# Attention and feed-forward on one core: the second batch's heads scored with queries on the partitions, one step per tile of the first feed-forward

## The chip, the cores and the metric

One of the NeuronCores of a Trainium2 chip runs the kernel. The metric is the device time of one execution in microseconds. The kernel before took 1074.35 us, the median of three runs (1073.28 to 1077.59).

## The reference

Eight batches of eight heads: 512 local queries attend to a window of 32 positions on either side and to 32 global keys, 32 global queries attend to everything. The heads of a batch laid side by side (512 columns) are the input of a feed-forward layer with a softplus.

```python
s_g = scale * np.matmul(q_g, k_all.transpose(0, 1, 3, 2))
out_g = np.matmul(sm(s_g), v_all)
...
mask = np.abs(pos[:, None] - pos[None, :]) <= window
s_ll = np.where(mask, s_ll, -1000000000.0)
s_lg = scale * np.matmul(q_l, k_g.transpose(0, 1, 3, 2))
a_l = sm(np.concatenate([s_lg, s_ll], axis=-1))
out_l = np.matmul(a_l, np.concatenate([v_g, v_l], axis=2))
...
h = x @ w_in                                    # 4352 x 512 by 512 x 2048
g = np.maximum(h, 0.0) + np.log1p(np.exp(-np.abs(h)))
out = g @ w_out                                 # 2048 x 512
```

The weights arrive as 64-bit floats and are split on the chip.

## The kernel before

**Feed-forward.** A batch's 512 local tokens go through 16 tiles of 128 columns of d_ff. Tile f of batch b is `h{b}_{f}`: four groups of three matmuls (high and low half of x, `xh` and `xl`, against the weights `wi`), then `act` (ScalarE takes the absolute value, the exponential and the logarithm; VectorE puts the softplus together in `e`; ScalarE casts its high half `gh`; GpSimd subtracts the low half `gl`). The second product adds tile f into four banks `o{b}_{t}` (three matmuls each, against `wo`), and it stands one or two tiles behind. The first product has a pool of two banks (`ps_h`), so that tile f + 2 waits until VectorE has read tile f.

**Weights.** The 32 weight tiles (`wi0` to `wi15`, `wo0` to `wo15`) come as raw 512 KB blocks and are split by `split_w`: ScalarE takes an absolute value (`wbits`), VectorE does four integer steps (L486, L488, L489, L492), ScalarE casts the high half, GpSimd subtracts the low half. Twelve are put out with the first batch's attention, the other twenty during the first feed-forward. A raw block lies in the SBUF tile of the next weight.

**Attention of the first batch** (pairs of heads m = 0 to 3) has the queries on the partitions. A step is half a pair, (m, a): `scores0` (mask and scores into two banks, `s0`), `soft0` (VectorE takes the maximum along the row and scales it, ScalarE does four exponentials with their sums), `invert0` and `diag0` (the reciprocals, put on a diagonal by ScalarE), `turn0` (eight matmuls that transpose and normalise at once, `t0`), `evict0` (ScalarE copies one half of `t0`, and then VectorE the other), `values0` (`o0_{m}_{a}`) and `split0`. After each two pairs comes a step for the global queries (`s0g`, `t0g`, `o0g`).

**Attention of all other batches** (m = 4 to 31) has the keys on the partitions: `scores` in three pieces (`s_ps`), a maximum by 32 x 32 transposes on VectorE (`mt`), `maxima` across partitions, a subtraction on GpSimd, an exponential, `values` (`v_ps`), and the sums' reciprocals by way of DRAM (`combine`, `invert`, `normalise`). For m below `MPE` the mask is added on TensorE and the scores are copied by ScalarE; from there on VectorE adds it while it copies.

**Order.** The pieces of m = 4 to 31 carry due times (12 per pair), and the feed-forward's items have due times of their own; pieces are put out between items. Pieces due before `START` come ahead of the first feed-forward. The scheduler then sets each engine's order. PSUM beside `ps_h`: a pool `ps_a` with one buffer of two banks (tag `a`), for `t0`, `v_ps` and later `s_ps`; and four banks `oA`, `oB` for the first scores, which become the four banks of the second product when that begins. Loads are issued in order by SyncE; the inputs of m = 4 among them ahead of the first feed-forward.

Of the kernel before, what the change touches and what calls it, by code (L numbers as in the profile page):

```python
# [31 lines left out]
MPE = 8  # L32
# [5 lines left out]
START = 69  # L38
# [15 lines left out]
def moe_over_global_local_attention(  # L54
# [28 lines left out]
    identf = pl.tile([P, P], F32, tag="e", name="identf", bufs=2)  # L83
# [4 lines left out]
    mask0 = pl.tile([P, 2, 2, 224], BF16, tag="rb", name="mask0", bufs=1)  # L88
# [47 lines left out]
    spare = [(kind, k) for k in range(NF - 1, 9, -1) for kind in ("wo", "wi")]  # L136

    def load0(m):
        for a, w in ((0, 704), (1, 832)):
            kind, k = spare.pop()  # L140
            t = pl.tile([P, w], F32, tag=f"{kind}{k}", name=f"raw0_{m}_{a}", bufs=1)
            order["load"] = nc.sync.dma_start(out=t, in_=qk0[m, :, 704 * a:704 * a + w]).ins
            st["raw0", m, a] = t
        kind, k = spare.pop()
        t = pl.tile([P, 4, 2, P], F32, tag=f"{kind}{k}", name=f"v0_{m}", bufs=1)
        order["load"] = nc.sync.dma_start(out=t, in_=v0[m].rearrange("p (c a d) -> p c a d", c=4, a=2)).ins
        st["v0", m] = t
# [7 lines left out]
    def exps0(shape, name):  # L155
        count0.append(name)
        tag = ("x", "wi9", "x", "wo9")[len(count0) % 4]
        return pl.tile(shape, F32, tag=tag, name=f"e0_{name}", bufs=2 if tag == "x" else 1)
# [45 lines left out]

    def evict0(m, a):
        v4 = st.pop(("t0", m, a)).rearrange("p h (c k q) -> p h c k q", c=2, k=2)
        t = st["p0", m, a] = [pl.tile([P, 2, 2, P], F32, tag=g, name=f"p0_{m}_{a}{g}", bufs=3) for g in ("gh", "gl")]
        keep("act", nc.scalar.copy(t[0], v4[:, :, :, 0]))
        keep("dve", nc.vector.tensor_copy(t[1][0:96], v4[0:96, :, :, 1]))

    def values0(m, a):
        t, vt = st.pop(("p0", m, a)), st["v0", m]
        ps = st["o0", m, a] = ps_h.tile([P, 512], F32, tag="h", name=f"o0_{m}_{a}").rearrange("p (c h q) -> p c h q", c=2, h=2)
        for c in range(2):
            for k, n in enumerate((P, 96)):
                mm(ps[:, c], lhsT=vt[:n, 2 * a + c, k], rhs=t[k][:n, :, c], start=k == 0, stop=k == 1, skip_group_check=True)

    def split0(m, a):
        ps = st.pop(("o0", m, a))
        if a == 0:  # L220
            xh[m] = pl.tile([P, 512], F32R, tag=f"xh{m}", name=f"xh0_{m}", bufs=1)
            xl[m] = pl.tile([P, 512], F32R, tag=f"xl{m}", name=f"xl0_{m}", bufs=1)
        hi, lo = ([x[m][r, 256 * a:256 * a + 256].rearrange("p (c q) -> p c q", c=2) for r in (slice(0, 64), slice(64, P))] for x in (xh, xl))
        part = [ps[64 * h:64 * h + 64, :, h] for h in range(2)]
        for h in range(2):
            keep("act", nc.scalar.copy(hi[h], part[h]))
        for h in range(2):
            keep("dve", nc.vector.tensor_tensor(lo[h], part[h], hi[h].bitcast(F32), op=ALU.subtract))  # L228


    def scores0g(n):
        ps = ps_s.tile([P, 2, 512], F32, tag=("oA", "oB")[n], name=f"s0g{n}")
# [16 lines left out]
    def evict0g(n):  # L249
        ps = st.pop(("t0g", n))  # L250
        t = st["p0g", n] = [pl.tile([P, 4, P], F32, tag=g, name=f"p0g{n}{g}", bufs=3) for g in ("gh", "gl")]
# [3 lines left out]
    def values0g(n):  # L255
        t = st.pop(("p0g", n))
        ps = st["o0g", n] = ps_h.tile([P, 512], F32, tag="h", name=f"o0g{n}")
# [6 lines left out]
    def split0g(n):  # L264
# [5 lines left out]
        nc.scalar.dma_start(out=xg_dram[2 * n:2 * n + 2, :, 0:SG].rearrange("j p q -> p j q"), in_=y)  # L270
# [3 lines left out]
    def load(m, p):  # L274
        w = QW[p] + KWID[p]
        raw = pl.tile([P, 544], F32, tag="raw", name=f"raw{m}_{p}", bufs=3)
        order["load"] = nc.sync.dma_start(out=raw[:, :w], in_=qk[m - M0, :, EW[p]:EW[p] + w]).ins
        st["raw", m, p] = raw

    def load_v(m):  # L280
        t = pl.tile([P, 2, 6, 66], F32, tag="v", name=f"v{m}", bufs=2)
        nc.gpsimd.memset(t[:, :, :, D:D + 1], 1.0)
        nc.sync.dma_start(out=t[:, :, :, 0:D], in_=v[m - M0].rearrange("p (h c d) -> p h c d", h=2, d=D))
        st["v", m] = t

    def scores(m, p):
        raw = st.pop(("raw", m, p))
        q = QW[p]
        if m < M0 + 2:
            ps = ps_s.tile([P, 2, 512], F32, tag=("oA", "oB")[(3 * m + p) % 2], name=f"s_ps{m}_{p}")  # L290
        else:
            ps = ps_a.tile([P, 2, 512], F32, tag="a", name=f"s_ps{m}_{p}")
        parts = ((0, 0, 192), (192, 96, 192 if p < 2 else 96))
        pe_mask = m < MPE
        masks = (mask[:, 0:192], mask[:, 192:384] if p < 2 else mask5)
        for i, (o, qs, w) in enumerate(parts):
            ks = q + 128 * i
            for h in range(2):
                r = slice(64 * h, 64 * h + 64)
                mm(ps[:, h, o:o + w], lhsT=raw[r, ks:ks + P], rhs=raw[r, qs:qs + w],  # L300
                   start=True, stop=not pe_mask, skip_group_check=True)
            for h in range(2 if pe_mask else 0):
                mm(ps[:, h, o:o + w], lhsT=ident, rhs=masks[i], start=False, stop=True, skip_group_check=True)
# [6 lines left out]
        if pe_mask:  # L310
            nc.scalar.copy(s, ps[:, :, 0:32 * nb])
        else:
            for o, mk in ((0, mask[:, 0:384]),) if p < 2 else ((0, mask[:, 0:192]), (192, mask5)):
                w = mk.shape[1]
                nc.vector.tensor_tensor(s[:, :, o:o + w], ps[:, :, o:o + w], mk.unsqueeze(1).to_broadcast([P, 2, w]), op=ALU.add)  # L315
# [95 lines left out]
    def pieces():  # L411
# [6 lines left out]
        for m in range(M0, M):  # L418
# [20 lines left out]
    def split_x(b, j):  # L439
        xh[j] = pl.tile([P, 512], F32R, tag=f"xh{j}", name=f"xh{b}_{j}", bufs=1)  # L440
        xl[j] = pl.tile([P, 512], F32R, tag=f"xl{j}", name=f"xl{b}_{j}", bufs=1)
        if b < B:
            assert (b, j) in ready
            t, seg = xa[b, j], SEG
# [67 lines left out]
    def moe_items():  # L512
# [70 lines left out]
        for i, (b, f) in enumerate(tiles):  # L583
            if f == 0 and b > 0:
                items.append((b, 0, 0, lambda b=b: [split_x(b, j) for j in range(4)]))
            w = 0 if b else 4 * f
# [20 lines left out]
    wk = [0, 0]  # L607

    def loads(upto):
        while wk[0] < min(upto, len(order_w)):  # L610
# [4 lines left out]
    def weights(upto):  # L615
        loads(upto + AHEAD)
        while wk[1] < min(upto, len(order_w)):
# [13 lines left out]
    pcs = pieces()  # L631
    local = (scores0, lambda m, a: invert0((m, a), 4), lambda m, a: diag0((m, a), 4), turn0, evict0, values0, split0)
    glob = (scores0g, lambda n: invert0(n, 1), lambda n: diag0(n, 1), turn0g, evict0g, values0g, split0g)
    steps = [(local, (m, a)) for m in range(M0) for a in range(2)]
    for at, n in ((6, 0), (9, 1)):
        steps.insert(at, (glob, (n,)))
    n = len(steps)
# [6 lines left out]
    for k in range(-2, n + 2):  # L644
        stage(k + 2, 0)

        while k >= n - 2 and pcs[0][0] < min(12 * M0 + 8 * (k - n + 3), START):
            pcs.pop(0)[1]()
# [13 lines left out]
        if -1 <= k and wk[1] < W_PRE:  # L662
            held = order_w[wk[1]]
            held += (abs_w(*held),)
            wk[1] += 1
    tight = False
# [18 lines left out]
def _layout(q_l, k_l, v_l, q_g, k_g, v_g):  # L685
# [21 lines left out]
    cols, va, vb = [], vl[:H].reshape(H, 4, P, D), np.zeros((H, 4, P, D), v_l.dtype)  # L707
    for c in range(4):
        x0 = P * c
        before = kl[:H, :, x0 - 32:x0] if c else pad[:H]  # L710
        behind = kl[:H, :, x0 + P:x0 + P + 32] if c < 3 else pad[:H]
        cols += [ql[:H, :, x0:x0 + P], kg[:H], before, behind, kl[:H, :, x0:x0 + P]]
        vb[:, c, 0:32] = vg[:H]
        if c:
            vb[:, c, 32:64] = vl[:H, x0 - 32:x0]
        if c < 3:
            vb[:, c, 64:96] = vl[:H, x0 + P:x0 + P + 32]
    g = np.zeros((H, D, 4, 32), q_l.dtype)
    for h in range(H):
        g[h, :, h % 4] = qg[h]  # L720
    qk0 = np.concatenate(cols + [g.reshape(H, D, P)], axis=2).reshape(M0, P, 1536)
    v0 = np.stack([va, vb], axis=2).reshape(M0, 2, 4, 2, P, D).transpose(0, 4, 2, 3, 1, 5).reshape(M0, P, 1024)
    return [np.ascontiguousarray(a) for a in (qk0, v0, qk[M0:], v[M0:])]
# [20 lines left out]
```

## Time and profile before

| | |
|---|---|
| median of 3 runs | 1074.35 us (1073.28 to 1077.59) |
| the profiled execution | 1076.06 us, span 1074.0 us |
| first matmul of the first feed-forward | 89.74 us |
| first matmul of the second feed-forward | 239.41 us |
| steady length of a batch (waits for `rb` of successive batches at 470.04 and 585.94 us) | 115.90 us |

An engine's line in the profile names the source line, the engine, the operation and the tiles (written from read). In a timeline the first number is the start in us from the span's start, the second the length; `x4` says that four equal instructions are merged, and the square bracket is the idle time ahead of it with what ended it. Matmuls are pipelined, so the distance from one start to the next tells what a group costs TensorE, and not its length. A matmul of 32-bit floats counts as two instructions.

### The profile page before, as it was taken

To read this page: it belongs to the slowest core of one execution; us is meant where nothing else is said; L and a number is where in the kernel's file an instruction comes from. 1 tells how busy PE (TensorE), PEld (TensorE's weight loads), DVE (VectorE), ACT (ScalarE), POOL (GpSimd) and SP (SyncE) were. 2 spreads that over 40 slices of the span, in tenths; PEclk is the share of its full clock that TensorE was granted. 3 is DMA by queue.
4 is the path that set the end of the run, shared out by engine and by line. 5 is a ranking of instruction groups with operands and counts; after the bars stand their busy time and mean duration, and the time that the engine had idled before them with its cause. 6 is when DMAs were issued, how large, how long until landed. Compare 5 with 4: busy or idle time off the path is not lost.

```text
span 1074.0 us, 14186 instructions
## 1 busy us (share of the span) xinstructions
PE 1016.3 (95%) x5108; PEld 803.7 (75%) x5108; DVE 593.4 (55%) x1138; ACT 556.2 (52%) x998; POOL 437.2 (41%) x496
## 2 busy tenths in 40 slices
PE   6895788898999999999999999999999999999996
PEld 4674566676777777777777777777777778888895
DVE  6988697965455655565545645565556542311111
ACT  6855555454445545455445544554455554554452
POOL 2236475642444444444434344444444441122221
PEclk8998889999999999999999999999999999999999
DMA  9532332312222221223212312131212210200010
GB/s 363 166 91 99 102 133 76 97 47 85 57 49 57 82 57 48 57 58 97 57 47 58 96 46 57 49 93 45 58 48 64 79 28 13 72 1 1 1 41 20
DMA packets 78566, 75.05 MB, mean 70 GB/s; under 512 B 53380, under 2 KB 57476, under 8 KB 78496
## 3 DMA queue, kind: packets, MB, share of 16 engines
q1 hardware_dynamic: 77952, 74.09, 23.3%
q8 instruction: 40, 0.66, 0.3%
q14 instruction: 30, 0.25, 0.1%
q10 hardware_dynamic: 544, 0.07, 0.0%
HBM read 64.43 MB, written 9.71 MB: 69 GB/s over the span
## 4 chain that ended last, share of the span: by engine, by line
PE 74%; DVE 7%; DMA 4%; issue 3%; POOL 2%; ACT 1%; POOLq 0%; ACTq 0%
PE h L126 31%; PE o L126 30%; PE v_ps L126 8%; PE s_ps L126 5%; DMA rb<-rec_scratch 2%; DVE xl L452 2%; DVE xa L404 1%; DMA rec_scratch<-sc 1%; POOL s L352 1%; DVE mt L316 1%; DVE s L315 1%; POOL wo L498 0%; DVE mb L347 0%; DVE wbitswo L489 0%; DVE wbitswo L486 0%
## 5 line engine op out<-in xcount | busy, mean ns | idle before, releaser
L126 PE MATMUL h<-xh,wi 128*128 128x512 f32 (+1 forms) x1152 | 357.4, 394 | 17.0 <-DVE xl L228 9.3
L126 PE MATMUL o<-wo,gh 128*128 128x512 f32 x1088 | 346.3, 400 | 0.0
L547 POOL TENSOR_TENSOR gl<-e,gh 128x512 fp32r<-128x512 f32 x136 | 177.2, 1303 | 397.2 <-ACT gh L546 340.4
L126 PEld LDWEIGHTS h<-xh,wi 128*128 128x128 f32 x1152 | 208.7, 190 | 65.3 <-issue 16.1
L126 PEld LDWEIGHTS o<-wo,gh 128*128 128x128 f32 x1088 | 201.6, 190 | 44.3 <-issue 4.0
L126 PE MATMUL h<-xl,wi 128*128 128x512 f32 (+1 forms) x576 | 220.9, 384 | 3.6 <-DVE xl L452 3.6
L126 PE MATMUL o<-wo,gl 128*128 128x512 f32 x544 | 214.2, 394 | 0.0
L540 ACT ACTIVATE e<-h 128x512 f32<-128x512 f32 x136 | 81.3, 598 | 254.9 <-PE h L126 252.6
L543 DVE SCALAR_TENSOR_TENSOR e<-h,e 128x512 f32<-128x512 f32 x136 | 93.2, 685 | 185.5 <-ACT e L542 185.5
L352 POOL TENSOR_TENSOR s<-s,mb 128x384 f32<-128x384 f32 x112 | 137.9, 1262 | 14.0 <-DVE mb L347 14.0
L126 PEld LDWEIGHTS h<-xl,wi 128*128 128x128 f32 x576 | 109.4, 190 | 28.4 <-DVE xl L452 6.4
L546 ACT CAST gh<-e 128x512 fp32r<-128x512 f32 x136 | 83.9, 617 | 89.7 <-DVE e L543 89.6
L126 PEld LDWEIGHTS o<-wo,gl 128*128 128x128 f32 x544 | 102.8, 189 | 22.9
L126 PE MATMUL v_ps<-s,v 128*65 128x192 f32 (+1 forms) x672 | 115.4, 315 | 3.0 <-DVE s L315 2.7
L315 DVE TENSOR_TENSOR s<-s_ps,mask 128x768 f32<-128x768 f32 (+1 forms) x96 | 64.9, 696 | 82.3 <-PE s_ps L126 82.3
L126 PEld LDWEIGHTS v_ps<-s,v 128*65 128x65 f32 x672 | 89.7, 138 | 26.5 <-DVE s L315 3.1
L542 ACT ACTIVATE e<-e,one 128x512 f32<-128x512 f32 x136 | 98.3, 723 | 3.3
L126 PE MATMUL s_ps<-raw 64*128 64x192 f32 (+1 forms) x672 | 79.0, 348 | 12.1 <-issue 8.0
L541 ACT ACTIVATE e<-e 128x512 f32<-128x512 f32 x136 | 85.5, 629 | 3.4
L356 ACT ACTIVATE s<-s 128x768 f32<-128x768 f32 (+1 forms) x84 | 66.0, 791 | 39.7 <-POOL s L352 24.7
L126 PEld LDWEIGHTS s_ps<-raw 64*128 64x128 f32 x672 | 53.4, 189 | 43.3 <-issue 34.1
L404 DVE TENSOR_TENSOR xa<-x,rb 64x608 f32<-64x608 f32 x56 | 71.0, 1268 | 22.8 <-DMA rb<-rec_scratch 22.4
(142 smaller groups left out, 817.4 us busy)
## 6 DMA issues: line engine op xcount, KB each, us to landing
raw<-in_qk SPq DMA_DIRECT2D x56, 272.0 KB
v<-in_v SPq DMA_DIRECT2D x28, 384.0 KB
out<-ot SPq DMA_DIRECT2D x34, 256.0 KB
rb<-rec_scratch SPq DMA_DIRECT2D x28, 304.0 KB
wiraw<-in_w_in SPq DMA_DIRECT2D x16, 512.0 KB
woraw<-in_w_out SPq DMA_DIRECT2D x16, 512.0 KB
raw<-in_qk SPq DMA_DIRECT2D x28, 224.0 KB
v<-in_v SPq DMA_DIRECT2D x4, 512.0 KB
```

Of the source, the lines that this page charges most:

```text
L126: order["pe"] = after(nc.tensor.matmul(*a, **k), "pe").ins
L315: nc.vector.tensor_tensor(s[:, :, o:o + w], ps[:, :, o:o + w], mk.unsqueeze(1).to_broadcast([P, 2, w]), op=ALU.add)
L352: nc.gpsimd.tensor_tensor(sw, sw, windows(mb[:, h], 0, 96, 2, 192), op=ALU.subtract)
L356: nc.scalar.activation(s, s, AF.Exp, scale=0.125)
L404: after(nc.vector.tensor_tensor(y[64 * h:64 * h + 64], x[0:64, h], rb[:, h], op=ALU.mult), "scores")
L452: nc.vector.tensor_tensor(lo, f(t), hi.bitcast(F32), op=ALU.subtract)
L540: nc.scalar.activation(e, ph, AF.Abs)
L541: nc.scalar.activation(e, e, AF.Exp, scale=-1.0)
L542: nc.scalar.activation(e, e, AF.Ln, bias=one)
L543: nc.vector.scalar_tensor_tensor(e, ph, 0.0, e, op0=ALU.max, op1=ALU.add)
L546: nc.scalar.copy(gh, e)
L547: nc.gpsimd.tensor_tensor(gl, e, gh.bitcast(F32), op=ALU.subtract)
```

## The change

The second batch's heads (m = 4 to 7) move from the second form of attention to the first. Ten more steps (eight halves of pairs and two global ones) join the list `steps`; each is put out in three parts, and one step is due per tile of the first feed-forward, from tile 0 on: scores, softmax and diagonal (`scores1`) at its tile, `turn1` one and a half tiles later, `values1` a quarter of a tile after that. `START` goes from 69 to 60; no attention of the second batch stands ahead of the first feed-forward. `values1` leaves its result in `xa`, 512 columns wide, and `split_x` takes it from there.

The new steps' `t0`, their values and, from m = 5 on, their scores all lie in the one buffer `a`. The raw inputs of m = 4 to 7 lie in tiles of weights that have not come yet (`wi15`, `wo15`, `wo14`) and in `v` and `rb`; so loads of weights from `wi14` on are held back by `gate` until the step (2,) has put out its values. The load of `wi14` needs the tile of m = 6's second raw half, whose last reader is the global step of m = 6 and 7. GpSimd's subtraction, the maxima and the way by DRAM fall away for m = 4 to 7, and the mask on TensorE in `scores` with them.

```diff
-START = 69
+START = 60
...
-        ps = ps_s.tile([P, 2, 512], F32, tag=("oA", "oB")[a], name=f"s0_{m}_{a}")
+        if m <= M0:
+            ps = ps_s.tile([P, 2, 512], F32, tag=("oA", "oB")[a], name=f"s0_{m}_{a}")
+        else:
+            ps = ps_a.tile([P, 2, 512], F32, tag="a", name=f"s0_{m}_{a}")
...
+    def bank(m, name):
+        return ps_h.tile([P, 512], F32, tag="h", name=name) if m < M0 else ps_a.tile([P, 2, 512], F32, tag="a", name=name)[:, 0]
...
-        pe_mask = m < MPE
...
-        for m in range(M0, M):
+        for u, (fs, arg) in enumerate(steps[n0:]):
+            at = START + (first + 48 - START) / NF * u
+            g = (first + 48 - START) / NF / 4
...
+            ps += [(at, scores1), (at + 6 * g, turn1), (at + 7 * g, values1)]
...
+        for m in range(MT, M):
...
-        while wk[0] < min(upto, len(order_w)):
+        while wk[0] < min(upto, order_w.index(("wi", NF - 2)) if gate else len(order_w)):
...
-    for p in range(NPC):
-        load(M0, p)
-    load_v(M0)
-    load_v(M0 + 1)
     loads(W_PRE + 2)
+    for m in range(M0, M0 + 2):
+        load0(m)
...
-        while k >= n - 2 and pcs[0][0] < min(12 * M0 + 8 * (k - n + 3), START):
-            pcs.pop(0)[1]()
```

On TensorE, in the kernel before, the second product of tile 1 of the first batch (`o0_0` to `o0_3`) holds a third of a pair's values between its halves.

```order
L126 MATMUL o0_0_1024<-wo1_543,gh0_1_949 128x512 x2
L126 MATMUL o0_0_1024<-wo1_543,gl0_1_950 128x512
L126 MATMUL o0_1_1028<-wo1_543,gh0_1_949 128x512 x2
L126 MATMUL o0_1_1028<-wo1_543,gl0_1_950 128x512
L126 MATMUL v_ps4_2_1112<-s4_2_723,v4_148 65x192
L126 MATMUL v_ps4_2_1112<-s4_2_723,v4_148 65x96
L126 MATMUL v_ps4_2_1112<-s4_2_723,v4_148 65x192
L126 MATMUL v_ps4_2_1112<-s4_2_723,v4_148 65x96
L126 MATMUL o0_2_1040<-wo1_543,gh0_1_949 128x512 x2
```

In the changed kernel most of the first tiles look like this one, tile 3's second product with the step (5, 1) around it; ahead of these rows stand the first product of tile 5 and, before that, the scores of the next step.

```order
L126 MATMUL t0_5_1_1207<-diag(5, 1)_1057,e0_5_1_1047 96x128
L126 MATMUL o0_0_918<-wo3_709,gh0_3_993 128x512 x2
L126 MATMUL o0_0_918<-wo3_709,gl0_3_994 128x512
L126 MATMUL o0_1_922<-wo3_709,gh0_3_993 128x512 x2
L126 MATMUL o0_1_922<-wo3_709,gl0_3_994 128x512
L126 MATMUL o0_5_1_1226<-p0_5_10_1216,v0_5_166 128x256
L126 MATMUL o0_5_1_1226<-p0_5_11_1217,v0_5_166 128x256
L126 MATMUL o0_5_1_1226<-p0_5_10_1216,v0_5_166 128x256
L126 MATMUL o0_5_1_1226<-p0_5_11_1217,v0_5_166 128x256
L126 MATMUL o0_2_934<-wo3_709,gh0_3_993 128x512 x2
```

A turn, its values and the next scores now stand in one round with a tile's two products, and all three use buffer `a`.

On VectorE, in the kernel before, the rows around the third tile's softplus (`e0_2`) mix weights with the keys-on-partitions attention (`x4` is the sum of values of pair 4, `mt6` the maxima of pair 6).

```order
L489 SCALAR_TENSOR_TENSOR wbitswi10_1167<-wiraw10_1009,wbitswi10_1167 128x512
L374 TENSOR_TENSOR x4_929<-x4_929,v_ps4_1_1032 65x2x64
L375 TENSOR_TENSOR x4_929<-x4_929,v_ps4_1_1032 65x2x32
L492 SCALAR_TENSOR_TENSOR woraw7_900<-woraw7_900,wbitswo7_1141 128x512
L543 SCALAR_TENSOR_TENSOR e0_2_1000<-h0_2_978,e0_2_1000 128x512
L492 SCALAR_TENSOR_TENSOR wiraw10_1009<-wiraw10_1009,wbitswi10_1167 128x512
L316 TENSOR_REDUCE mt6_971<-s6_1_1075 128x2x12
```

In the changed kernel the rows behind `e0_2` are these, up to VectorE's half of the first turned probabilities (`p0_4_01`).

```order
L541 SCALAR_TENSOR_TENSOR wbitswo7_1071<-woraw7_782,wbitswo7_1071 128x512
L544 SCALAR_TENSOR_TENSOR woraw7_782<-woraw7_782,wbitswo7_1071 128x512
L179 TENSOR_SCALAR sums4_1_845<-sums4_1_845 128x4
L538 TENSOR_SCALAR wbitswi11_1172<-wbitswi11_1172 128x512
L180 RECIPROCAL sums4_1_845<-sums4_1_845 128x4
L540 TENSOR_SCALAR wbitswi11_1172<-wbitswi11_1172 128x512
L541 SCALAR_TENSOR_TENSOR wbitswi11_1172<-wiraw11_971,wbitswi11_1172 128x512
L538 TENSOR_SCALAR wbitswi12_1294<-wbitswi12_1294 128x512
L544 SCALAR_TENSOR_TENSOR wiraw11_971<-wiraw11_971,wbitswi11_1172 128x512
L540 TENSOR_SCALAR wbitswi12_1294<-wbitswi12_1294 128x512
L541 SCALAR_TENSOR_TENSOR wbitswi12_1294<-wiraw12_1095,wbitswi12_1294 128x512
L225 COPY p0_4_01_911<-t0_4_0_901 96x512
```

Between VectorE's last split of the first batch's x (`xl0_3`) and this copy stand 50 rows: 39 steps of weights (`wo8`, `wi7`, `wo4`, `wi8`, `wi9`, `wo5`, `wo6`, `wo7`, `wi11` whole, three of `wi12`), the maxima, scalings, sums and reciprocals of the steps (4, 0) and (4, 1), and `e0_0`, `e0_1`, `e0_2`. In the kernel before, the same stretch (to `e0_2`) had maxima of pairs 4 to 6 between its weights.

More of the change, by code (lines that the diff above doesn't have):

```diff
@@ L31 @@
 M0 = 4
-MPE = 8
+MT = 8
 LAG = 22
@@ L219, in split0 @@
         ps = st.pop(("o0", m, a))
+        if m >= M0:
+            b, j = divmod(m, H // 2)
+            if a == 0:
+                xa[b, j] = pl.tile([P, 608], F32, tag="xa", name=f"xa{b}_{j}", bufs=4)
+            else:
+                ready.add((b, j))
+            for h, (what, f) in enumerate((("act", nc.scalar.copy), ("dve", nc.vector.tensor_copy))):
+                rows = slice(64 * h, 64 * h + 64)
+                keep(what, f(xa[b, j][rows, 256 * a:256 * a + 256].rearrange("p (c q) -> p c q", c=2), ps[rows, :, h]))
+            return
         if a == 0:
@@ L276, in load @@
         raw = pl.tile([P, 544], F32, tag="raw", name=f"raw{m}_{p}", bufs=3)
-        order["load"] = nc.sync.dma_start(out=raw[:, :w], in_=qk[m - M0, :, EW[p]:EW[p] + w]).ins
+        order["load"] = nc.sync.dma_start(out=raw[:, :w], in_=qk[m - MT, :, EW[p]:EW[p] + w]).ins
         st["raw", m, p] = raw
@@ L300, in scores @@
                 mm(ps[:, h, o:o + w], lhsT=raw[r, ks:ks + P], rhs=raw[r, qs:qs + w],
-                   start=True, stop=not pe_mask, skip_group_check=True)
-            for h in range(2 if pe_mask else 0):
-                mm(ps[:, h, o:o + w], lhsT=ident, rhs=masks[i], start=False, stop=True, skip_group_check=True)
+                   start=True, stop=True, skip_group_check=True)
         if p == 0:
```

119 lines of the change are left out of this document (74 added, 45 removed).

## The prediction

> **What bounds the kernel now.** I read the page first, then the busy time by stage, then the timelines of TensorE and VectorE where TensorE stands still.
>
> ```profile
> PE 1016.3 (95%) x5108; PEld 803.7 (75%) x5108; DVE 593.4 (55%) x1138; ACT 556.2 (52%) x998; POOL 437.2 (41%) x496
> ...
> PE   6895788898999999999999999999999999999996
> ...
> PEclk8998889999999999999999999999999999999999
> ```
>
> TensorE is the bound of the whole, but not of its first quarter, where slices 4 to 9 are not full and the granted clock falls to 0.8. The next view splits the span where the first feed-forward's third tile is done (108.9 us) and where the third tile of the second feed-forward starts (255.1 us). Columns: stretch, length, busy time (and count) of TensorE, weight loads, VectorE, ScalarE and GpSimd, granted clock, share and rate of the DMA engines.
>
> ```profile
> 59.30:108.90 49.60, 38.59 (x231) 28.73 (x230) 43.12 (x75) 27.83 (x50) 25.77 (x28) 0.90 0.33 103
> 108.90:255.10 146.20, 124.78 (x580) 94.14 (x580) 112.77 (x189) 79.36 (x136) 79.10 (x78) 0.91 0.30 92
> 255.10:371.00 115.90, 115.20 (x579) 90.54 (x577) 65.75 (x130) 58.29 (x99) 50.86 (x60) 1.00 0.24 62
> ```
>
> From 255.1 us on TensorE is never short of work, and its rows from there (tile `h1_2`, after pair 10's second scores) are the same in both kernels. So the change is worth what it does to the arrival at this point. Up to there, VectorE is the fullest engine beside TensorE: 43.1 of 49.6 us in the first stretch. Five rows of TensorE mark the places.
>
> ```profile
> 59.31 0.60 PE L126 MATMUL s_ps<-raw 64*128 64x192 f32 x4
> ...
> 89.74 1.19 PE L126 MATMUL h<-xh,wi 128*128 128x512 f32 x2 [9.25 <-DVE xl L228]
> ...
> 97.23 0.72 PE L126 MATMUL h<-xh,wi 128*128 128x512 f32 x2 [1.75 <-ACT yg L269]
> ...
> 108.51 0.39 PE L126 MATMUL o<-wo,gl 128*128 128x512 f32 x1
> ...
> 255.11 0.73 PE L126 MATMUL h<-xh,wi 128*128 128x512 f32 x2
> ```
>
> At 59.31 us the first scores of pair 4 start, from here the kernels differ. The first feed-forward then waits 9.25 us for the last split of x, which VectorE reaches late. The 89.74 row is also a price: the same two matmuls take 1.19 us after that wait and 0.72 us later, so a long wait costs some 2 us more in slow matmuls.
>
> **TensorE's work, removed and added.** Distances from one start to the next in the first batch give the price of a step.
>
> ```profile
> 28.58 0.54 PE L126 MATMUL s<-mask,ident 128*128 128x448 bf16 x2
> ...
> 30.01 0.70 PE L126 MATMUL o<-p_1gh,v 128*128 128x256 f32 x2
> ...
> 31.85 1.93 PE L126 MATMUL t<-diag(1, 1)_328,e 128*128 128x128 f32 x16
> 33.61 1.03 PE L126 MATMUL s0g<-raw,raw 128*128 128x256 f32 x4
> ...
> 35.70 0.68 PE L126 MATMUL o<-p_0gh,v 128*128 128x256 f32 x2
> ...
> 62.40 1.03 PE L126 MATMUL o0g<-p0g0gh,v 128*128 128x64 f32 x8
> ...
> 65.12 2.03 PE L126 MATMUL t<-diag(3, 1)_590,e 128*128 128x128 f32 x16
> ...
> 71.72 1.39 PE L126 MATMUL t0g<-diag,e_g 128*128 128x128 f32 x10
> 73.04 0.60 PE L126 MATMUL s_ps<-raw 64*128 64x192 f32 x4
> ```
>
> Scores 1.43, values 1.84, a turn 1.76 (with its load 1.86), so 5.1 us for half a pair; a global step 2.09 + 1.32 + 2.72 = 6.1. Added: 8 x 5.1 + 2 x 6.1 = 53 us. Removed: two masked pieces of `s_ps` took from 59.31 to 62.40, so 12 pieces 18.5 us; a `v_ps` takes the 1.17 us below, so 12 take at most 14.0, and 13.2 with the third piece of each pair taken as a fifth shorter. Together 31.7. TensorE has **21.5 us more** to do.
>
> ```profile
> 134.40 1.46 PE L126 MATMUL v_ps<-s,v 128*65 128x192 f32 x8
> 135.57 0.76 PE L126 MATMUL h<-xh,wi 128*128 128x512 f32 x2
> ...
> 228.16 2.74 PE h L126 x12
> ```
>
> A tile's product (12 matmuls) takes 2.74 us; I use 2.77. Counted from 59.3 to the common point: 18 first and 16 second products 94.2; the first batch's rest 12.3 (1.9 + 2 x 1.84 + 2 x 2.72 + 1.3); scores of pairs 8 to 10 and two values of pair 8, 8.7. With the new steps 168.5 us, with the old pieces 147; the kernel before took 195.8, so 49 us are there to hide the 21.5. That is the case for the change. The question is whether VectorE lets it happen.
>
> **VectorE ahead of the first turn.** VectorE has a queue in fixed order, and the order shows 50 rows between the last `xl0_3` and its half of the first `t0` of pair 4. What follows in TensorE's queue, `o0_4_0`, the next scores, `h0_3` and all the rest, waits for that copy. The price of a weight, alone and beside GpSimd:
>
> ```profile
> 33.70 0.41 DVE L486 TENSOR_SCALAR wbitswi<-wbitswi 128x512 f32<-128x512 f32 x1
> 34.15 0.43 DVE L488 TENSOR_SCALAR wbitswi<-wbitswi 128x512 int32<-128x512 int32 x1
> 34.61 0.69 DVE L489 SCALAR_TENSOR_TENSOR wbitswi<-wiraw,wbitswi 128x512 int32<-128x512 int32 x1
> 35.34 0.69 DVE L492 SCALAR_TENSOR_TENSOR wiraw<-wiraw,wbitswi 128x512 int32<-128x512 int32 x1
> ...
> 60.98 0.69 DVE L209 COPY p_0gl<-t 96x512 f32<-96x512 f32 x1
> ...
> 75.78 0.28 DVE L253 COPY p0g1gl<-t0g 32x128 f32<-32x128 f32 x1
> ...
> 88.74 0.85 DVE L228 TENSOR_TENSOR xl<-o,xh 64x256 fp32r<-64x256 f32 x2
> ...
> 101.10 0.69 DVE L543 SCALAR_TENSOR_TENSOR e<-h,e 128x512 f32<-128x512 f32 x1
> ...
> 103.07 1.52 DVE L486 TENSOR_SCALAR wbitswo<-wbitswo 128x512 f32<-128x512 f32 x1
> 104.63 1.42 DVE L488 TENSOR_SCALAR wbitswo<-wbitswo 128x512 int32<-128x512 int32 x1
> ```
> ```profile
> 104.26 1.50 POOL L498 TENSOR_TENSOR wi<-wiraw,wi 128x512 fp32r<-128x512 f32 x1
> ```
>
> Alone a weight takes 0.45 + 0.46 + 0.73 + 0.65 = 2.3 us; beside a GpSimd subtraction a 0.43 us step takes 1.42 us, so each of GpSimd's rows can cost VectorE about a microsecond. [...]
>
> From 60.98 us, where the copy of the first batch's seventh turn starts in either kernel, to the end of `xl0_3` stand three weights, three copies (0.69, 0.69, 0.28) and four halves of x (0.43 each): 3.4 us and three weights at 2.8 to 3.2, some 12.5 us. So the first feed-forward can start at about **73.5 us instead of 89.7**: the 9.25 us wait goes. But then the 39 steps of weights (9.75 weights) and 11 others follow (three `e` of 0.69, two maxima of 1.1, six small ones of 0.2: 5.2 us): 9.75 x 2.8 + 5.2 = 32.5, so the copy starts at **106 us**. Both ends: 2.3 us a weight gives 101, 3.2 (every weight three contended steps) 110; I take 2.8, since GpSimd's queue holds twelve rows of 1.3 to 1.5 us in these 33 us. By then TensorE has done three first products, one turn, two scores and half a second product, 14 of 33 us, and waits at `h0_2` (for `e0_0`) and at `o0_4_0`. In the kernel before it had at 108.9 us three first products and one second, with seven pieces of scores and two of values. So the late start of the old kernel is not won, it turns into a wait behind weights.
>
> **From there on.** Left for TensorE: 168.5 - 26.7 = 141.8 us in the changed kernel, 110.3 in the kernel before, which took 146.2. The waits I add come from the one buffer `a`: after scores end, VectorE's maximum and scaling and ScalarE's exponentials must be through before the next turn may write.
>
> ```profile
> 43.92 1.08 DVE L164 TENSOR_REDUCE sums<-s 128x4 f32<-128x896 f32 x1
> 45.03 0.17 DVE L165 TENSOR_SCALAR sums<-sums 128x4 f32<-128x4 f32 x1
> ```
> ```profile
> 45.29 0.45 ACT L167 ACTIVATE e<-s,sums 128x224 f32<-128x224 f32 x1 [1.25 <-DVE sums L165]
> ...
> 47.00 0.74 ACT L226 CAST xh<-o 64x256 fp32r<-64x256 f32 x2
> ...
> 48.25 1.27 ACT L181 ACTIVATE diag(3, 0)_538<-identf,sums 128x128 f32<-128x128 f32 x4
> ```
>
> That is 1.37 + 1.71 us and about 0.2 of handing over, 3.3 us, of which a first product covers 2.75: 0.55 us in each of nine rounds, **5 us**. The other dependencies of a round fit: ScalarE's absolute value, diagonal (1.27) and exponential, then its and VectorE's copies (VectorE's 0.69, ScalarE's about the same) end 6.9 us after the scores, where TensorE arrives at 6.6. If VectorE or ScalarE had a weight in the way, each round would lose up to a weight's 2.3 us; the order has weights in three rounds, **1.5 us**. GpSimd in the way of the scaling: **2 us**. The load of `wi14` can start only after the last global scores, and ScalarE's queue waits for it ahead of the copies of `t0_7_1`.
>
> ```profile
> 191.37 3.61 DMA wiraw<-in_w_in
> ```
>
> With 3.6 us for that load, 1.7 on ScalarE and 3.3 of weights on VectorE, `t0_7_1` is copied 8.1 us after those scores, and pair 8's first scores stand 2.3 us, their successors 2.6 us: **5 us**. The slow restart after the long wait **2**, the tail (pair 8's exponentials behind `wo15`'s split) **3.5**. On SyncE the raw inputs of pairs 6 and 7 are asked for two rounds ahead, and cost nothing unless a load takes over 20 us.
>
> Sum: 106 + 141.8 + 19 = 267 against 255.1, **12 us later**. The profiled execution took 1076.06 us, 0.2% over the median of the runs, so I add 12.2 to the median: **1087 us**.
>
> **Rivals.** (1) *TensorE hides it all.* VectorE runs at its pace alone (copy at 101 us) and the rounds lose nothing but the 0.55: 101 + 141.8 + 5 + 3 = 251, 4 us earlier, 1070; with the first matmuls at full clock and no load in the way 1066. For it: GpSimd is relieved and VectorE has little to do after 110 us (11 weights, the rest is under 60 us of 150). It decides where the copy comes before 102 us or the later waits stay under 8. Against it: twelve rows of GpSimd still lie beside those weights. The middle of the two, 1071 to 1079, is the tie. (2) *The clock.* The rounds' short waits bring the clock down: the row after the 9.25 us wait costs 1.19 for 0.72. If each round had 3 us at half clock, 1.5 us x 9 = 13 more, 1100. Against it: after 1.75 us of idling (the 97.23 row) the matmuls ran at full pace. [...] (3) *The steps do not stand one per tile*, and the values pile up at the end: the order rules this out, they do.
>
> **How the numbers follow.** Forecast (1079 to 1098) 0.5; tie (1069 to 1079) 0.24; rival 1 in full (below 1069) 0.14; rival 2 (above 1098) 0.12. A measurement here tells about 0.5% (5.4 us) from no change. Slower by more: 0.5 + 0.12 = 0.62; same 0.24; faster 0.14. The range reaches from rival 1's end, 1066, to rival 2's with its copy at 110 us, 1102.
>
> **What would show it.** Right: the first `h` row near 73 us; a wait of 8 to 12 us in front of `o0_4_0`, released by VectorE's copy (L225) near 106; the rounds 11 to 12 us apart with waits for ScalarE's exponentials; `h1_2` near 267. Wrong: the copy before 100 us (weights cheaper than 2.3), or rounds of 10.6 us, TensorE's bare work, or of 14, and the granted clock below 0.9 through the rounds.

## The result, and the profile after

The changed kernel takes **1108.78 us** (median of 4 runs, 1107.75 to 1111.25), the kernel before 1073.82 us on the same chip; the ratio is 1.0315 (95% interval 1.0288 to 1.0342). That is 35 us slower, where the prediction said 12 us slower and at most 1102 us. The direction was right, the size was not.

The page of the changed kernel, lines as shown of before:

```profile
PE 1052.1 (95%) x5224; PEld 830.2 (75%) x5224; DVE 573.3 (52%) x1104; ACT 567.0 (51%) x1082; POOL 404.2 (36%) x452
...
PE   6894999898999999999999999999999999999996
...
PEclk9996999898999999999999999999999999999999
```

VectorE and GpSimd were relieved (VectorE 593.4 to 573.3 us, GpSimd 437.2 to 404.2), and TensorE is busy for 36 us more. Now the stages of busy time, cut at the start of the first values of pair 4 (109.2 us), at the end of the second global values (232.3) and at the common point (285.8); columns as in the prediction.

```profile
59.30:109.20 49.90, 33.23 (x173) 26.32 (x172) 47.05 (x76) 32.54 (x75) 20.07 (x14) 0.82 0.31 107
109.20:232.30 123.10, 111.12 (x547) 85.05 (x547) 50.27 (x91) 59.86 (x150) 26.30 (x22) 0.93 0.22 67
232.30:285.80 53.50, 48.67 (x222) 37.28 (x221) 36.77 (x63) 27.15 (x46) 26.34 (x29) 0.91 0.20 64
...
sum 226.50, PE 193.03 PEld 148.65 DVE 134.09 ACT 119.55 POOL 72.72; mean PE 64.34 PEld 49.55 DVE 44.70 ACT 39.85 POOL 24.24
```

The common point is reached at 285.8 us, 30.7 us later than before (255.1). From 59.3 us on TensorE was busy for 193.0 us and idle for 33.5; before, by the prediction's two stages, busy for 38.59 + 124.78 = 163.4 and idle for 32.4. **Idling has not shrunk, and the busy time grew by 29.7 us.** Behind the common point 821.8 us are left, against 818.9 before: 2.9 us more, so that the two profiled spans lie 33.6 us apart (1107.6 and 1074.0). The two rows of that stretch, the changed kernel's first:

```profile
285.80:1107.60 821.80, 812.54 (x4026) 646.14 (x4024) 394.67 (x770) 404.65 (x678) 318.71 (x359) 1.00 0.19 51
```
```profile
255.10:1074.00 818.90, 806.70 (x4026) 645.10 (x4024) 391.62 (x770) 405.60 (x678) 319.40 (x359) 1.00 0.19 52
```

With the same 4026 matmul records at the same granted clock TensorE is busy for 5.8 us more in the changed kernel, and idle for 2.9 us less (9.3 against 12.2). Why the same matmuls take 0.7% longer was not found.

TensorE's timeline at the places the prediction spoke of:

```profile
75.26 0.70 PE L126 MATMUL h<-xh,wi 128*128 128x512 f32 x2
...
86.17 1.22 PE L126 MATMUL h<-xh,wi 128*128 128x512 f32 x2 [3.76 <-DVE e L595]
...
95.23 3.62 PE L126 MATMUL t<-diag(4, 0)_771,e 128*128 128x128 f32 x16 [3.57 <-ACT diag(4, 0)_771 L187]
100.64 0.73 PE L126 MATMUL o<-wo,gh 128*128 128x512 f32 x2 [1.78 <-ACT e L173]
...
109.21 3.78 PE L126 MATMUL o<-p,v 128*128 128x256 f32 x8 [6.75 <-DVE p L225]
112.43 1.42 PE L126 MATMUL o<-wo,gh 128*128 128x512 f32 x2
113.64 0.63 PE L126 MATMUL o<-wo,gl 128*128 128x512 f32 x1
...
115.35 0.69 PE L126 MATMUL s<-mask,ident 128*128 128x448 bf16 x2
...
152.71 0.54 PE L126 MATMUL s<-mask,ident 128*128 128x448 bf16 x2 [2.38 <-DVE xa L244]
...
212.89 0.92 PE L126 MATMUL s_ps<-raw 64*128 64x192 f32 x8 [3.08 <-DVE p L225]
215.46 3.78 PE L126 MATMUL o<-p,v 128*128 128x256 f32 x8 [1.65 <-DVE s L335]
...
267.62 2.79 PE L126 MATMUL v_ps<-s,v 128*65 128x192 f32 x8 [4.83 <-DVE s L335]
...
285.78 0.74 PE L126 MATMUL h<-xh,wi 128*128 128x512 f32 x2
```

The 9.25 us wait at 89.74 us is gone, and between 82 and 109 us stand four waits, 15.9 us together, of which the last is for VectorE's copy of the first `t0`. Look also at the lengths behind a wait: values that take 2.0 us at 146.93 us take 3.78 at 109.21 and at 215.46.

```profile
146.93 2.00 PE L126 MATMUL o<-p,v 128*128 128x256 f32 x8
```

The granted clock in stretches of 3.4 us behind two of the waits, the last but two columns in these rows (0.50, 0.55, 1.00 and 0.61, 0.88):

```profile
109.20:112.60 3.40, 3.39 (x9) 2.77 (x9) 1.05 (x1) 0.67 (x1) 1.79 (x2) 0.50 0.00 0
112.60:116.00 3.40, 3.40 (x11) 1.97 (x10) 0.43 (x1) 0.37 (x1) 0.00 (x0) 0.55 0.00 0
116.00:119.40 3.40, 3.40 (x20) 2.68 (x20) 1.26 (x2) 0.96 (x5) 0.00 (x0) 1.00 0.02 5
...
152.40:155.80 3.40, 3.09 (x12) 2.01 (x12) 3.11 (x6) 0.66 (x1) 1.60 (x1) 0.61 0.00 0
155.80:159.20 3.40, 3.32 (x14) 2.38 (x14) 1.41 (x5) 2.24 (x9) 0.25 (x1) 0.88 0.00 0
```

So these waits have a second price behind them (values of 3.78 us for 2.00, at a granted clock of 0.50), and the experiments have to separate three things: the waits for VectorE, the slow matmuls behind waits, and the added TensorE work itself.

### The profile page after: what moved, and what is told of

Read it like the earlier page. It is cut to its first block, busy times and chain, and to the rows that moved or that the text cites. A ratio compares the mean times of both kernels' runs of the same rounds, so it can differ in the third digit from the quotient of the medians.

```text
span 1107.6 us, 14379 instructions
## 1 busy us (share of the span) xinstructions
PE 1052.1 (95%) x5224; PEld 830.2 (75%) x5224; DVE 573.3 (52%) x1104; ACT 567.0 (51%) x1082; POOL 404.2 (36%) x452
## 3 DMA queue, kind: packets, MB, share of 16 engines
HBM read 63.69 MB, written 9.67 MB: 66 GB/s over the span
## 4 chain that ended last, share of the span: by engine, by line
PE 82%; DVE 9%; ACT 3%; DMA 3%; issue 1%; POOL 0%; SPq 0%; ACTq 0%; DVEq 0%; POOLq 0%
PE o L126 34%; PE h L126 31%; PE v_ps L126 8%; PE s_ps L126 5%; ACT e L173 1%; DMA wiraw<-in_w_in 1%; PE t L126 1%; DVE sums L170 1%; DVE wbitswo L538 1%; DVE woraw L544 1%; DMA v<-in_v 1%; DVE wbitswo L541 1%; DVE wbitswi L541 1%; PE o0g L126 1%; PE s L126 1%
## 5 line engine op out<-in xcount | busy, mean ns | idle before, releaser
L126 PE MATMUL o<-wo,gh 128*128 128x512 f32 x1088 | 352.4, 405 | 1.8 <-ACT e L173 1.8
L126 PEld LDWEIGHTS h<-xl,wi 128*128 128x128 f32 x576 | 108.9, 189 | 22.9
L372 POOL TENSOR_TENSOR s<-s,mb 128x384 f32<-128x384 f32 x96 | 119.0, 1269 | 1.5 <-DVE mb L367 1.5
L126 PE MATMUL v_ps<-s,v 128*65 128x192 f32 (+1 forms) x576 | 99.3, 316 | 4.9 <-DVE s L335 4.8
L126 PEld LDWEIGHTS v_ps<-s,v 128*65 128x65 f32 x576 | 76.5, 138 | 26.9 <-issue 5.2
L394 DVE TENSOR_TENSOR x<-x,v_ps 65x128 f32<-65x128 f32 x48 | 13.6, 284 | 119.4 <-ACT x L393 119.4
L424 DVE TENSOR_TENSOR xa<-x,rb 64x608 f32<-64x608 f32 x48 | 64.1, 1336 | 18.5 <-DMA rb<-rec_scratch 18.2
L376 ACT ACTIVATE s<-s 128x768 f32<-128x768 f32 (+1 forms) x72 | 56.4, 790 | 25.9 <-POOL mt L329 14.2
L126 PEld LDWEIGHTS s_ps<-raw 64*128 64x128 f32 x576 | 45.1, 186 | 29.4 <-issue 22.3
```

The costliest lines, as they stand in the source:

```text
L126: order["pe"] = after(nc.tensor.matmul(*a, **k), "pe").ins
L372: nc.gpsimd.tensor_tensor(sw, sw, windows(mb[:, h], 0, 96, 2, 192), op=ALU.subtract)
L376: nc.scalar.activation(s, s, AF.Exp, scale=0.125)
L424: after(nc.vector.tensor_tensor(y[64 * h:64 * h + 64], x[0:64, h], rb[:, h], op=ALU.mult), "scores")
```

## The experiments

Each time stands beside runs of the kernel before on the same chip (medians 1073.8 to 1074.3 us). The changed kernel was measured in the first comparison alone, so a difference to its 1108.78 us is one between chips.

**1. VectorE's weights tied back (hold).** The scheduler puts weights' steps wherever it thinks VectorE idle, so weights due later stand ahead of the copy. One line ties each late weight behind the attention step ahead of it in the program:

```diff
-        note("dve", i) if tight else after(i, "maxima")
+        note("dve", i) if tight else after(after(i, "maxima"), "dve")
```

> The changed kernel; nothing is left out. A late weight's first VectorE step is tied behind the attention step that precedes it in the program, so six of the 9.75 weights ahead of VectorE's copy of the first t0 of pair 4 move behind it. Theory V (the time is lost because TensorE waits for VectorE's weights, and each such wait is followed by matmuls at half clock): the copy comes at about 92 us instead of 108.5, the waits of 3.8, 3.6, 1.8 and 6.8 us of TensorE between 83 and 110 us mostly go, some of it comes back where the weights now lie in the rounds; 8 to 16 us off, 1093 to 1101. Theory T (TensorE's 21.5 us of added work and the single buffer a set the time, the weights only fill what would be idle): under 4 us off, 1105 to 1109.

Measured: 1090.95 us, **17.8 us less**, a little more than the 8 to 16 expected. The stages, and the row of the first values (cut at the same three places of this kernel):

```profile
59.30:98.40 39.10, 31.56 (x174) 25.11 (x172) 31.14 (x53) 28.25 (x69) 13.06 (x10) 0.90 0.39 136
98.40:219.80 121.40, 109.83 (x546) 84.36 (x546) 60.19 (x115) 62.75 (x156) 30.64 (x26) 0.94 0.23 69
219.80:267.60 47.80, 46.92 (x222) 36.13 (x221) 33.75 (x63) 26.57 (x46) 26.05 (x29) 0.96 0.20 63
```
```profile
98.37 3.78 PE L126 MATMUL o<-p,v 128*128 128x256 f32 x8 [4.30 <-DVE p L225]
```
```profile
97.62 0.69 DVE L225 COPY p<-t 96x512 f32<-96x512 f32 x1 [2.28 <-ACT p L224]
```
```profile
94.83 0.66 ACT L549 CAST wo<-woraw 128x512 fp32r<-128x512 f32 x1 [2.75 <-DVE woraw L544]
```

The first values come 10.8 us earlier, the middle is 1.7 and the tail 5.7 us shorter. The copy comes at 97.6 us and not at 92. VectorE waits 2.28 us of that for ScalarE's half of the same `t0`, and ScalarE comes to it late because its cast of a weight waits 2.75 us for VectorE's last step of this weight: weights that are left still stand in the way, now by way of ScalarE. Theory V holds for about half of the loss; the other half is still there.

**2. Cheaper weights in both kernels (light_after, light_before).** Two of a late weight's four steps on VectorE are left out, the maximum and the low three bits; these are the lines that fall away for late weights:

```diff
-        i = nc.vector.tensor_scalar(a.bitcast(F32), a.bitcast(F32), TINY, None, op0=ALU.max)
...
-        note("dve", nc.vector.scalar_tensor_tensor(r, lo32, 29, a, op0=ALU.logical_shift_right, op1=ALU.bitwise_or))
```

> The changed kernel with two of the four VectorE steps left out for every weight from the thirteenth on (the maximum and the low three bits), so such a weight costs VectorE 1.1 us alone instead of 2.3. Theory V: the first turn's copy comes some 12 to 15 us earlier, the splits of the two last weights cost less; 12 to 20 us off, 1089 to 1097. Theory T: under 4 us off.

> The kernel before with the same two steps left out for the same weights. Theory V: the kernel before has its long wait ahead of the first feed-forward, before most late weights, so it gains clearly less than the changed kernel, 2 to 8 us, 1066 to 1072, and the gap between the two shrinks from 34 us to about 20 or less. Theory T: the gap stays within 4 us of 34.

Measured: 1089.45 us (19.3 less than the changed kernel) and 1063.11 us (11.2 less than before). The changed kernel gains more, but the gap only shrinks from 35 to 26.3 us: neither theory as written. VectorE's weights hold up the old kernel too, more than the 2 to 8 us that I expected.

**3. More TensorE work in the kernel before (pe_before).** Ten matmuls ahead of each of ten first products:

```diff
                 g["ps", b, f] = t
+                if b == 0 and f < 10:
+                    for i in range(10):
+                        mm(t, lhsT=wi[f // 2 * 2][:, 0, 0:P], rhs=xh[0][:, 0:512], start=True, stop=True, skip_group_check=True)
```

> The kernel before with ten more matmuls 128x512 ahead of each of the first ten tiles' first product (their result is overwritten), 100 x 0.23 = 23 us of TensorE work, a little over what the change adds. Theory V: the kernel before has 49 us of waits and slow matmuls there, so about half or more is hidden: 3 to 12 us more, 1077 to 1086. Theory T: the work is paid: 18 to 23 us more, 1092 to 1097.

Measured: 1093.74 us, **19.5 us more**. The page has TensorE busy for 1039.5 us, 23.2 more than before:

```profile
PE 1039.5 (95%) x5208; PEld 822.9 (75%) x5208; DVE 592.2 (54%) x1138; ACT 556.6 (51%) x998; POOL 434.1 (40%) x496
```

So 84% of the work is paid although TensorE stands idle for 32 us in that stretch. Theory T is right here, and my reading that the waits "are there to hide" work is wrong: the wait of 9.25 us stays (9.22 in this run), because it ends when VectorE ends. This run has a limit: the added matmuls write into the bank of the tile that they stand in front of, so they wait for that bank as the tile does. What work placed inside a wait would cost is another question, and experiment 7 asks it.

```profile
90.76 4.59 PE L126 MATMUL h<-xh,wi 128*128 128x512 f32 x12 [9.22 <-DVE xl L228]
```

**4. Both kernels without the second batch's attention (bare_after, bare_before).**

```diff
             def scores1(fs=fs, arg=arg):
-                for f in (0, 1, 2):
-                    fs[f](*arg)
...
-        for m in range(M0, M):
+        for m in range(8, M):
```

> The changed kernel without the computation of the second batch's ten attention steps (their loads, the gate and everything else stay; x of the second batch is a constant). TensorE then has 115 us of work from 59.3 us to the common point in place of 168.5. Theory P (after the first runs: TensorE's added work is paid nearly in full, and what the kernel before has in waits is no cover for it): this kernel and the one below come to nearly the same time, about 1005 to 1025, and what the ten steps cost in place is 85 to 100 us for 53 us of matmuls. Theory C (the rest of the changed kernel, its loads and its weights' order, is itself slower): this kernel is over 8 us slower than the one below.

> The kernel before without the attention of pairs 4 to 7, the second batch's (loads, scores, maxima, probabilities, values and scaling; x of the second batch is a constant). Theory P: about 1005 to 1025, so that the old form costs 50 to 65 us in place for 31.7 us of matmuls, and the two forms differ by 30 to 38 us in place. Theory C: over 8 us faster than the kernel above.

Measured: 1030.16 and 1030.22 us, the same (the range of times expected was too low, the equality is theory P's). So `START`, the places of the loads and the gate cost nothing in sum while the ten steps are away: the difference lies in the two forms of attention where they stand. Two small differences work against each other in this. The point from which 4026 matmul records are left lies at 205.7 us in the bare changed kernel and at 209.5 in the other, and TensorE is busy for 812.1 and 806.9 us behind it. The rows show it too: the fourth group of the next first product starts 9.68 us behind this point in the changed kernel and 9.67 in its bare form, and 9.60 in both of the others. So the slower matmuls behind the common point do not come from the ten steps. The old form costs 44.1 us in place, the new one 78.6, both under what was expected (50 to 65 and 85 to 100). Against the prediction's estimates of their matmuls, 31.7 and 53 us, both cost more than their work, by 12 and 26 us. Between 75 and 150 us even the bare kernel waits for VectorE (group of all first products in that window, its idle time behind the bar):

```profile
L126 PE MATMUL h<-xh,wi 128*128 128x512 f32 x80 | 31.6, 482 | 13.7 <-DVE e L590 12.1 <-DVE xl L254 1.5
```

**5. The last weights' gate opened later (hold_gate).**

```diff
-                    gate.clear()
+                if arg == (M0 // 2 + 1,):
+                    gate.clear()
```

> The run hold (late weights tied behind the attention step before them) with the gate of the last weight loads opened one step later, behind the second global step's values, so that no split of wi14 stands ahead of the copies of t0_7_1. The weight wi14 is needed some 20 us after that. Theory V: the waits of 3.1, 1.1 and 1.1 us in front of pair 8's first pieces and the half clock behind them (the window from 200 to 225 us has a granted clock of 0.73) go: 5 to 9 us under hold, 1082 to 1086. Rival: the load only moves its wait to the tail: within 3 us of hold, 1088 to 1094.

Measured: 1097.58 us, 6.6 us more than hold. The wait of 3.1 us in front of pair 8's scores went, and the tail got a larger one, for pair 8's exponentials. They wait for GpSimd's subtraction, which stands behind that of `wo15`, and this one waits 7.18 us for the late split (TensorE's row, then GpSimd's):

```profile
254.76 2.82 PE L126 MATMUL v_ps<-s,v 128*65 128x192 f32 x8 [10.60 <-ACT s L376]
```
```profile
248.31 1.27 POOL L551 TENSOR_TENSOR wo<-wlastwo,wo 128x512 fp32r<-128x512 f32 x1 [7.18 <-ACT wo L550]
...
251.89 3.86 POOL L372 TENSOR_TENSOR s<-s,mb 128x384 f32<-128x384 f32 x4
```

The rival has the mechanism, though not the size (it said within 3 us of hold): the gate's wait is moved, and grows.

**6. The like tie in the kernel before (hold_before).** Here a late weight is tied behind the scores step ahead of it:

```diff
-        note("dve", i) if tight else after(i, "maxima")
+        note("dve", i) if tight else after(after(i, "maxima"), "scores")
```

> The kernel before with its late weights tied, likewise, behind the attention's scores step that precedes them in the program; nothing is left out. Two of the weights ahead of the first e move back. Theory V: 2 to 7 us faster than before, 1067 to 1072, by the wait of 4.2 us ahead of the second piece of pair 8's forerunner. Rival (VectorE has no slack later in the kernel before, 77% busy there): within 2 us of before or slower.

Measured: 1067.78 us, a ratio of 0.9933 (0.9906 to 0.9961) to the kernel before, and so **faster than both kernels**, by 0.7% against the kernel before. TensorE's wait of 4.18 us there (118.54) is one of 2.03 here (112.72). With both orders tied, the forms stand 1090.95 - 1067.78 = 23.2 us apart, close to the 21.5 us of TensorE work that the prediction counted as added. That this work is the reason is not shown: experiment 8 finds only half of such work paid in hold.

**7. Keeping TensorE busy in a wait (warm_after).** 24 useless matmuls, whose result is overwritten, in the 6.75 us wait:

```diff
             def values1(fs=fs, arg=arg):
+                if arg == (M0, 0):
+                    t = early[2] = output_banks().tile([P, 512], F32, tag="o2", name="o0_2")
+                    for i in range(24):
+                        mm(t, lhsT=wi[0][:, 0, 0:P], rhs=xh[0], start=True, stop=True, skip_group_check=True)
```

> The changed kernel with 24 matmuls 128x512 (5.5 us, their result is overwritten) in front of o0_4_0, where TensorE waits 6.75 us for VectorE's copy. They lengthen no wait, they only keep TensorE busy in it. Theory K (a wait is followed by matmuls at half clock, which cost time of their own): o0_4_0 takes 2.0 us instead of 3.8 and the six matmuls behind it 2.75 instead of 5.1 us, so 2 to 4 us off, 1105 to 1107. Rival (the slow rows behind a wait are not caused by the idling of TensorE, or they are absorbed in the next wait): within 1 us of the changed kernel, 1108 to 1110, or more where the added matmuls themselves run late.

Measured: 1102.47 us, **6.3 us less with more work**. At the place itself:

```profile
103.38 6.26 PE L126 MATMUL o<-xh,wi 128*128 128x512 f32 x24
109.47 1.89 PE L126 MATMUL o<-p,v 128*128 128x256 f32 x8
111.01 0.81 PE L126 MATMUL o<-wo,gh 128*128 128x512 f32 x2
111.67 0.39 PE L126 MATMUL o<-wo,gl 128*128 128x512 f32 x1
...
112.58 0.55 PE L126 MATMUL s<-mask,ident 128*128 128x448 bf16 x2
```

The values start 0.26 us later than in the changed kernel (109.21) and take 1.89 instead of 3.78 us; the next scores start at 112.58 instead of 115.35, 2.8 us earlier. **The slow matmuls behind this one wait cost 2.8 us, and idling was their cause.** The 6.3 us aren't the clock's alone: the scheduler also gave VectorE another order at the end of the first feed-forward, of the kind that the last experiment tries by itself.

**8. Work and weights on top of hold (pe_hold, light_hold).** The edits of 3 and 2 in the kernel of 1.

> The run hold with ten more matmuls 128x512 ahead of each of the first ten tiles' first product, as in the run pe_before (23 us of TensorE work). Theory P (with VectorE's weights out of the way, TensorE is itself the bound of the rounds, and the waits that are left are not cover for more): 18 to 24 us over hold, 1109 to 1115. Rival (what is left beside TensorE's work hides more of it): 4 to 14 us over, 1095 to 1105.

> The run hold with the two VectorE steps of each late weight left out too, as in the run light_after. Theory V (the two runs took away the same wait, that for the first copy): little over either alone, 0 to 6 us under hold, 1085 to 1091. Rival (the weights cost VectorE's time everywhere, not at that place): the sum of the two gains, 15 us or more under hold, 1076 or less.

Measured: 1102.79 us (11.8 over hold) and 1086.84 us (4.1 under it). Here half of the 23 us does not show in the time, so the rival held for the work. The stretch up to the common point, in hold and then in pe_hold, tells where it went:

```profile
59.30:267.60 208.30, 188.31 (x940) 145.61 (x938) 125.09 (x230) 117.57 (x271) 69.75 (x64) 0.93 0.25 80
```
```profile
59.30:279.20 219.90, 204.67 (x1039) 161.21 (x1039) 124.72 (x230) 120.23 (x271) 69.55 (x64) 0.96 0.24 76
```

TensorE is idle for 4.8 us less (15.2 against 20.0), so that much fits into the waits. But it is also busy for only 16.4 us more, and not for 23, at a granted clock of 0.96 instead of 0.93: the larger part comes back because fewer matmuls are slow (from the granted clocks, some 0.07 x 208.3 = 14.6 us are lost in hold and 0.04 x 219.9 = 8.8 in pe_hold, an estimate). Cheaper weights bring little more once the order is right, as theory V said: both edits took away the same wait.

**9. The tail alone (tail_after).** Three splits of the second batch's x stand behind the copy of pair 9's third scores, not ahead:

```diff
-            nc.vector.tensor_tensor(lo, f(t), hi.bitcast(F32), op=ALU.subtract)
+            i = nc.vector.tensor_tensor(lo, f(t), hi.bitcast(F32), op=ALU.subtract)
+            if b == 1 and j >= 1:
+                after(i, "third9")
```

> The changed kernel; nothing is left out. On VectorE three of the second batch's four splits of x (xl1 to xl3 of the second feed-forward) are tied behind the maxima of pair 9's third scores, where the changed kernel has them ahead of the masked copy of these scores; the orders of TensorE and GpSimd stay as they are, on ScalarE two neighbours swap. In the trace of the changed kernel TensorE waits 4.83 us there, in front of pair 8's first values, and the rows behind that run at half clock for 5 us. Theory K (the tail costs the wait and the slow rows behind it): the copy comes some 4 us earlier; 4 to 7 us off, 1102 to 1105. Rival (the splits are needed so soon for the second feed-forward's first product that the wait moves there): under 2 us off, 1107 to 1110.

Measured: 1104.54 us, 4.2 us less. In the changed kernel VectorE's rows there are:

```profile
261.13 5.50 DVE L504 TENSOR_TENSOR xl<-xa,xh 128x512 fp32r<-128x512 f32 x4
266.56 0.81 DVE L335 TENSOR_TENSOR s<-s_ps,mask 128x384 f32<-128x384 f32 x2
```

and with the edit TensorE's pair 8 values come 6.1 us earlier and at full pace, 1.49 us for 2.79 (2.3 us of this the profiled execution, the fastest of the five, already has at the scores ahead of them, 256.67 us against 259.01):

```profile
261.53 1.49 PE L126 MATMUL v_ps<-s,v 128*65 128x192 f32 x8 [1.07 <-DVE s L335]
```

## Why the prediction was wrong in size

By its own steps, against the trace of the changed kernel:

- *First feed-forward at 73.5 us*: 75.26. Right within 2 us.
- *Copy of the first `t0` at 106 us (101 to 110) behind 50 rows*: it starts at 108.47, the values at 109.21. The mechanism is right, and hold shows it. A weight cost (108.47 - 75.14 - 5.2) / 9.75 = 2.9 us, where I took 2.8. (The eleven other rows add up to 5.5 us at the prices given, not to 5.2; the result is the same.)

```profile
75.14 1.57 DVE L538 TENSOR_SCALAR wbitswo<-wbitswo 128x512 f32<-128x512 f32 x1
...
108.47 0.68 DVE L225 COPY p<-t 96x512 f32<-96x512 f32 x1
```

- *Waits from there on, 17 us without the restart*: idle time is 123.10 - 111.12 = 12.0 up to the end of the global values and 53.50 - 48.67 = 4.8 behind it, 16.8 together. The sum is right, in part by luck: its parts are not all where I put them. The tail's is due to the four splits of x, which I had not seen, and not to `wo15`.
- *141.8 us of TensorE work*: busy time is 159.8 us. At granted clocks of 0.93 and 0.91 up to 8.6 + 4.8 = 13.4 us of it are lost to the clock (an estimate, and an upper bound: a part of the time at a lower clock is idle time, as in the second half of the 4.83 us wait, where the granted clock is 0.63 from 265.20 to 267.62 us). 146.4 are left, 4.6 more than my count.
- *"The slow restart after the long wait 2"*: **this is the term that failed.** It should have been 12 to 13, since it was put behind one wait and there are five places with slow matmuls from 109 us on. Together with 3.2 for the later start and 4.6 for the work that gives the missing 19 us (266.8 predicted, 285.8 measured).

What hid it from me was in my own rows: the kernel before ran at 0.91 over 146 us from 108.9 us on, by the same estimate 13 us lost to slow matmuls, and I compared its whole stretch with a sum for the changed kernel that had nearly full clock. The rival on the clock had the mechanism but put it behind the wrong waits. Waits of 0.33 to 0.34 us in four rounds, and two of 0.92 and 1.24 us (189.76 and 171.90), cost nothing behind them (granted clock 1.00 from 120 to 150, from 171.90 to 178.70 and from 175 to 200 us):

```profile
125.00:150.00 25.00, 24.52 (x128) 19.50 (x126) 9.84 (x20) 13.66 (x34) 6.25 (x5) 1.00 0.34 119
...
175.00:200.00 25.00, 23.41 (x121) 17.44 (x120) 7.12 (x15) 12.84 (x37) 2.54 (x2) 1.00 0.04 12
```

It is the waits of 2.38 to 6.75 us, and what follows them closely, that have half clock behind them (a granted clock of 0.50 in the 3.4 us from 109.20, from 216.29 and from 267.62 us; and one wait of 1.06 us, at 229.20, with 0.63 from 232.60 to 236.00), and I dismissed them by one row (1.75 us, granted clock 1.00 from 97.23 to 100.60).

Of the three causes, the runs show: VectorE's order ahead of the first turn and in the tail (17.8 us by hold, of which the tail alone is about 4), slow matmuls behind one wait (2.8 us), and added work that is largely paid (84% in the kernel before, half in hold, where it won back slow matmuls). These overlap, since a wait taken away takes its slow matmuls with it (as in experiment 9), and they can't be added. That the rest of the slow matmuls, some 9 to 10 us, has the same cause as those of experiment 7 is argued from the granted clock, not tried place by place.

## What to carry to other kernels

Idle time of the bound engine is not by itself room for more work: ask what ends each wait, because one that ends with another engine's queue stays when work is added behind it (the wait of 9.25 us was one of 9.22, and 19.5 of 23.2 us were paid). When a stage is estimated as work plus waits, carry over its granted clock too, since behind each of the 43 waits of 2.44 us or more in these traces matmuls run at half clock within 5 us (0.50 in the 3.4 us behind the 6.75 us wait). And where a scheduler fills gaps, look for steps that are due late and stand ahead of a copy that TensorE needs: one tie behind the right step was worth 17.8 us here, and 6.5 in the kernel before.

## What the hardware showed beside

Useless matmuls made the kernel faster (1102.47 against 1108.78 us): 24 of them in a wait (6.26 us in the trace) took 2.8 us off the rows behind it. A wait of 2.38 us (152.71) was followed by a granted clock of 0.61 in the next 3.4 us. The same wait in warm_after (2.38 us) was followed by full clock (1.00 from 150 to 175 us): the row of the first product behind these scores takes 0.73 us there (151.22), and 1.22 in the changed kernel (154.97).

```profile
149.79 0.54 PE L126 MATMUL s<-mask,ident 128*128 128x448 bf16 x2 [2.38 <-DVE xa L244]
```

Counted over the 14 traces of this case, from 59 us to 260 us in the two bare kernels and to 340 us in the others, half clock (rows 1.6 to 2.5 times as long as the same rows elsewhere) lies within 5 us behind each of TensorE's 43 waits of 2.44 us or more, and behind 8 of the 11 from 2.0 to 2.4 us. In the changed kernel it lies behind waits of 6.75 and 4.83 us, and behind less as well (2.38 us at 152.71, 1.06 us at 229.20). In the run hold, there were three waits of 3.11, 1.06 and 1.06 us; the rows are slow behind the first two, and again for some 7 us behind the third:

```profile
200.46 1.65 PE L126 MATMUL s_ps<-raw 64*128 64x192 f32 x8 [3.11 <-DVE p L225]
203.18 3.78 PE L126 MATMUL o<-p,v 128*128 128x256 f32 x8 [1.06 <-DVE s L335]
...
215.85 4.04 PE L126 MATMUL o0g<-p0g,v 128*128 128x64 f32 x20 [1.06 <-DVE s L335]
219.81 1.22 PE L126 MATMUL o<-wo,gh 128*128 128x512 f32 x2
...
224.58 0.62 PE L126 MATMUL h<-xh,wi 128*128 128x512 f32 x2
```

So a wait of about 1 us, which cost nothing in the rounds (0.92 and 1.24 us), can be followed by half clock as well (1.06 us); what decides it was not tried.
